# The channel loop of an attention and state-space backward pass: another order for the first roundings, the exponentials and the correlation copies, and two Toeplitz tiles

## The chip, the cores and the metric

The kernel runs on one core of a Trainium2 chip. A core has engines that each work through a queue of their own and meet through semaphores: TensorE (PE: matrix products, with the loading of weights shown apart as PEld), VectorE (DVE), ScalarE (ACT), GpSimd (POOL), and SyncE (SP), which here issues the DMAs. On-chip memory is SBUF; matrix products land in PSUM, which is cut into 8 banks of 128 x 512 fp32 values. The metric is the device time of one execution in microseconds (us), the median of several.

## The reference

A block mixes attention (without a causal mask) and a state-space convolution (S4) with a gate per token; asked for are its value and the gradients of twelve of its inputs, given grad_out. Everything but the S4 parameters is bfloat16. Cut to what is computed:

```python
def fwd(x, wqkv, wo, A, Bc, Cc, log_dt, Dskip, gate_w):    # A, Bc, Cc complex [576, 128]
    g = sigmoid((x * gate_w).sum(-1, keepdims=True))
    q, k, v = heads(x @ wqkv)                                # 2048 tokens, 32 heads of 18
    a = merge(softmax(q @ k.T * 18**-0.5) @ v) @ wo
    dt = exp(log_dt)
    K = real(sum_n(Cc * exp(dt * A * l) * (dt * Bc)))        # l = 0..2047, one K per channel
    y = causal_convolution(u, K) + u * Dskip                 # u: its own input, with x's data
    return g * a + (1 - g) * y
out, vjp = jax.vjp(fwd, ...)
return (out, *vjp(grad_out))
```

Here u is a constant: the gradient through it isn't asked for.

## The kernel before

The program has five stages: projections and preparation, attention forward and backward, the attention gradients' last products, the S4 part (from L708 on), and a final stage that puts the outputs together. The change touches the S4 part and, for one row, the final stage.

**What the S4 part computes.** The sequence of 2048 is cut into 16 pieces of 128 positions. Per channel there are 128 complex modes. For each channel the powers exp(dt A l), l from 0 to 127, are made as a 128 x 128 table E1e (real and imaginary part). With it, TensorE turns the inputs and the gated output gradients of each piece into states (uvp, copied to UV), a recurrence over the 16 pieces carries states forward and adjoint states backward (HG), a second product brings them back to positions (ybp), and what happens inside a piece is a Toeplitz product with the channel's kernel (T0w). Sums over products of states (pairs1, pairs2) give the parameter gradients, and the correlation of x with the output gradient inside a piece goes along two further columns of RX into the same states.

**How it is staged.** The 576 channels go in NBLK = 18 blocks of CB = 32, each block in two halves (h = 0, 1) of GS = 16 channels, and each half in 4 groups (q) of 4 channels, since 4 channels x 128 modes fill one PSUM bank. The loop is a software pipeline: `for i in range(-1, NBLK + 1)` works in one iteration on the recurrence of block i, the tables of block i + 1, the Toeplitz part of block i - 1, the masks and correlation products of block i + 3 (`mb`) and their collection for block i + 2 (`sb`).

The functions that the prediction names:

- `phase` (L856): one matmul `ph` of 3 rows of split phases (`thr`) with the positions (`lrow`), into one of three PSUM banks with the tag "ph".
- `ex` (L863): per half four phases, each turned to its exponential `ab` by ScalarE (L867). The exponentials need another function table than the roundings before them (ACT_TABLE_LOAD). Both halves of block i + 2 are made at the end of iteration i, into the two `ab` tiles.
- `kk` (L869): a phase, which ScalarE rounds by adding the constant MAGIC (L874). `ff` (L876): VectorE subtracts phase and rounding, which leaves the fraction of a turn. The phase's bank is free only after that. There is one `kk` tile.
- `sn` (L881): sine and cosine of the fractions on ScalarE. `prod` (L889): the products E1e of these with `ab` on VectorE (L892, L893), and a DMA transpose to E1n.
- `uv` (L897): the state matmuls uvp into two banks with the tag "uv", copied to UV by ScalarE.
- `scan` (L913): the recurrence HG on VectorE, 15 steps. It begins with a cast (L918), with which one iteration is told from the next in the trace.
- `kp` (L967): the Toeplitz kernel's row of every channel, stored to Kp_d. `t0` (L1013): per half the load of T0w from Kp_d (L1023), 16 matmuls `tps` into the bank with the tag "tm", and on VectorE the sum `yd` (L1028) with `ydi`.
- `load_rx`, `prep_rx` (L776, L784): for every second block the load of the columns RX and of `gob`, and three products by VectorE (L786, L788, L789).
- `m_load` (L791): the load of `xs` and `gyp` for the correlation, and 7 copies of xs shifted by 1 to 7 partitions, from SBUF to SBUF (L796). `m_mask` (L798): their masks on VectorE (L801). `m_part` (L803): products `psM`, also in the bank "tm", copied by ScalarE to `mst` (L812) and stored to Md_d by four DMAs each. `m_skw` (L823): four skewed loads from Md_d. `m_sum` (L831): four matmuls with `sel` into the bank "misc". `m_fin` (L836): three copies by ScalarE of the result, the last into the row dDs_row.
- `pairs2` (L996): products by VectorE (pq, rr), summed by TensorE over k with an identity, also into "misc" (58 matmuls `misc<-rr,ident_bf`). `sums` (L1010): ScalarE's copy SS of the result.

Of the 8 banks, "ph" has three, "uv" two, and "misc", "ybp" and "tm" one each.

**What sets the order.** On TensorE, ScalarE, VectorE and GpSimd the order is that of the program text (L770). The DMAs of SP are put in order by the framework's scheduler, and each waits in SP's queue until what it reads is there and what it overwrites is free.

Of the kernel before, what the change touches and what calls it, by code (L numbers as in the profile page):

```python
# [10 lines left out]
ACT = mybir.ActivationFunctionType  # L11
BF = mybir.dt.bfloat16
F32 = mybir.dt.float32
# [4 lines left out]
P = 128  # L18


def build(tc, aps, dbg_aps=None, stages=("s1", "attn", "post", "s4", "final")):
    nc = tc.nc
# [16 lines left out]
    S, D = x2.shape  # L39
# [21 lines left out]
    with ExitStack() as gctx:  # L61
# [27 lines left out]
        N = A_re.shape[1]  # L89
# [618 lines left out]
        if "s4" in stages:  # L708
            CB = 32
# [5 lines left out]
            s4c = s4c_cm.__enter__()  # L715
            SS = s4c.tile([P, 6, D], F32, name="SS")
            CK = s4c.tile([P, 2, 2, D], BF, name="CK")
            dDs_row = s4c.tile([1, D], F32, name="dDs_row")
            ones_f = s4c.tile([P, 1], BF, name="ones_f")
            nc.vector.memset(ones_f, 1.0)  # L720

            with ExitStack() as ctx:
# [80 lines left out]
                def m_part(b, u):  # L803
                    d0 = b * CB
                    psM = pps.tile([P, 4, P], F32, tag="tm", name="psM")
                    for q in range(4):
                        for g_ in range(4):
                            dd = u * 16 + 4 * q + g_
                            mm(psM[32 * g_:32 * (g_ + 1), q, :].rearrange("p (a b) -> p a b", b=SUB), lhsT=gyp[:, :, dd],
                               rhs=xs[:, :, ::-1, dd], tile_position=(0, 32 * g_))  # L810
                    mst = mst2[u]
                    nc.scalar.copy(mst[:, :, 0:P], psM)  # L812
                    for g_ in range(4):
                        dst = Md_d[d0 + u * 16:d0 + (u + 1) * 16].rearrange("(q g) t w -> g t q w", g=4)
                        nc.sync.dma_start(dst[g_], mst[32 * g_:32 * g_ + SUB, :, :])
# [20 lines left out]
                def m_fin(b):  # L836
                    RX = RXs[b // 2][0]
                    o = (b % 2) * CB
                    pk = dkp(b)
                    nc.scalar.copy(RX[:, CDK, o:o + CB], pk)  # L840
                    nc.scalar.mul(RX[:, CDK + 1, o:o + CB], pk, l0col)
                    nc.scalar.copy(dDs_row[:, b * CB:(b + 1) * CB], pk[0:1, :])

                def blk(b):
                    if b not in BK:
# [7 lines left out]
                                nc.sync.dma_start(t_[32 * (1 - r_):32 * (1 - r_) + 3, :], spl_d[r_, :, dG:dG + GS, :].rearrange("q d n -> q (d n)"))  # L853
                    return BK[b]

                def phase(b, h, q, which):  # L856
                    B_ = blk(b)
                    r0 = 32 * which
                    ph = pps.tile([P, 4, N], F32, tag="ph", bufs=3, name="ph")
                    mm(ph.rearrange("p c n -> p (c n)"), lhsT=lrow[r0:r0 + 3, :], rhs=B_["rw"][h][r0:r0 + 3, q * 4 * N:(q + 1) * 4 * N], tile_position=(r0, 0))  # L860
                    return ph

                def ex(b, h):  # L863
                    B_ = blk(b)
                    ab = B_["ab"][h] = pw.tile([P, GS, N], F32, tag="ab", bufs=2, name="ab")
                    for q in range(GS // 4):
                        nc.scalar.activation(ab[:, 4 * q:4 * q + 4, :], phase(b, h, q, 1), ACT.Exp)  # L867

                def kk(b, h, q):  # L869
                    B_ = blk(b)  # L870
# [142 lines left out]
                def t0(b, h):  # L1013
# [3 lines left out]
                        ydx[b // 2] = pw.tile([P, 2, NB, XB], BF, tag="yd", name="yd")  # L1017
                    yd = ydx[b // 2]
                    RX = RXs[b // 2][0]
                    T0w = pw.tile([P, GS, P], BF, tag="T0w", name="T0w")  # L1020
                    dh = b * CB + h * GS
                    src = bass.AP(tensor=Kp_d.tensor, offset=Kp_d[dh:dh + 1, 1:2].offset, ap=[[1, P], [2 * P, GS], [1, P]])
                    nc.sync.dma_start(T0w, src)  # L1023
# [21 lines left out]
                m_fin(0)  # L1045
                m_part(1, 0)
                m_part(1, 1)
                for i in range(-1, NBLK + 1):
                    cur = 0 <= i < NBLK
                    nx = i + 1 < NBLK  # L1050
                    mb = i + 3 if i + 3 < NBLK else None
                    sb = i + 2 if i + 2 < NBLK else None
                    if mb is not None:
                        m_load(mb)
                    if nx:
                        kk(i + 1, 0, 0); kk(i + 1, 0, 1)
                    if cur:
                        scan(i, 0, 3)
                    if nx:
                        ff(i + 1, 0, 0); kk(i + 1, 0, 2)  # L1060
                    if sb is not None:
                        m_skw(sb)
                    if cur:
                        scan(i, 3, 5)
                    if nx:
                        ff(i + 1, 0, 1); kk(i + 1, 0, 3)
                    if cur:
                        scan(i, 5, 7)
                    if nx:
# [6 lines left out]
                    if cur:  # L1076
                        scan(i, 9, 15)
                        casts(i)
                        rw1(i)
                    if sb is not None and sb % 2 == 0:  # L1080
                        load_rx(sb // 2)
                    if i >= 1:
                        t0(i - 1, 0)
                        t0(i - 1, 1)
                    if sb is not None and sb % 2 == 0:
                        prep_rx(sb // 2)
                    if nx:
                        prod(i + 1, 0)
                        kk(i + 1, 1, 0); kk(i + 1, 1, 1); kk(i + 1, 1, 2)
# [13 lines left out]
                        kp(i)  # L1103
                    if mb is not None:
                        m_mask(mb)
                    if nx:
                        prod(i + 1, 1)
                        uv(i + 1, 1)
                    if cur:
                        pairs2(i)  # L1110
                    if sb is not None:
                        m_sum(sb)
                        m_fin(sb)
                    if i + 2 < NBLK:
                        ex(i + 2, 0)
                        ex(i + 2, 1)
                    if cur:
# [7 lines left out]
        if "final" in stages and "s4" in stages:  # L1125
            out0_v = aps_out["out_0"][0].rearrange("(t p) d -> p t d", p=P)
            out1_v = aps_out["out_1"][0].rearrange("(t p) d -> p t d", p=P)
            with ExitStack() as ctx:
# [84 lines left out]
                nc.vector.tensor_copy(rowb, row)  # L1213
                nc.sync.dma_start(aps_out["out_10"].rearrange("(o d) -> o d", o=1), rowb)
                rowb2 = pf.tile([1, D], BF, name="ddsrowb")
                nc.vector.tensor_copy(rowb2, dDs_row)
                nc.sync.dma_start(aps_out["out_11"].rearrange("(o d) -> o d", o=1), rowb2)

# [105 lines left out]
```

## Time and profile before

| | |
|---|---|
| time, median of 3 runs | 4279.74 us (4272.59 to 4279.76) |
| the profiled execution's own time | 4279.8 us |
| its span, first to last instruction | 4278.1 us |
| granted TensorE clock, mean | 0.561 |
| busy in the span: PE, DVE, ACT | 3258.8, 2934.7, 2930.1 us |
| the loop from the first HG cast to the last | 2986.75 to 4053.64 us of the span |
| DMA traffic over the span | 521 MB, mean 122 GB/s |

The page gives, of one execution, the busy time of each engine, the span in 40 slices, the DMA queues, and the costliest groups of instructions. The slices show the stages: the span up to slice 27 of 40 is attention and the products behind it, the rest the S4 part and the final stage. Each digit is a busy share in tenths:

```
PE   8979999999999999999999999693334344334311
DVE  5527767777777777677677778022767767767878
```

In the trace's views, a group row has a line, an engine, an operation and its tiles (out<-in), the count, the busy time and mean length, and the idle time of the engine just ahead of it with what ended it. A row of the list of waits says who waited for whom, the sum, how often, and the longest. In a timeline each row has a start, a length, and in brackets the idle time ahead.

### The profile page before, as it was taken

To read this page: it belongs to the slowest core of one execution; us is meant where nothing else is said; L and a number is where in the kernel's file an instruction comes from. 1 tells how busy PE (TensorE), PEld (TensorE's weight loads), DVE (VectorE), ACT (ScalarE), POOL (GpSimd) and SP (SyncE) were. 2 spreads that over 40 slices of the span, in tenths; PEclk is the share of its full clock that TensorE was granted. 3 is DMA by queue.
4 is the path that set the end of the run, shared out by engine and by line. 5 is a ranking of instruction groups with operands and counts; after the bars stand their busy time and mean duration, and the time that the engine had idled before them with its cause. 6 is when DMAs were issued, how large, how long until landed. Compare 5 with 4: busy or idle time off the path is not lost. (4 is left out here: it accounts for less than half of the span.)

```text
span 4278.1 us, 64835 instructions
## 1 busy us (share of the span) xinstructions
PE 3258.8 (76%) x24562; PEld 1156.9 (27%) x24562; DVE 2934.7 (69%) x5147; ACT 2930.1 (68%) x5340; POOL 21.7 (1%) x45
## 2 busy tenths in 40 slices
PE   8979999999999999999999999693334344334311
PEld 2312222222222222222222222362223223223310
DVE  5527767777777777677677778022767767767878
ACT  4469989989989899899899897013555455455501
POOL 0000000000000000000000000000000000000000
PEclk9855555555555555555555555795555555555555
DMA  7446777677777767776767777774454444454347
GB/s 196 144 100 122 126 137 119 126 136 122 124 136 122 134 129 124 135 125 124 137 122 120 129 120 137 208 180 81 80 95 88 87 89 86 86 95 85 71 124 174
DMA packets 1789270, 521.42 MB, mean 122 GB/s; under 512 B 1702074, under 2 KB 1767684, under 8 KB 1788956
## 3 DMA queue, kind: packets, MB, share of 16 engines
q1 hardware_dynamic: 1788956, 517.27, 62.6%
q8 instruction: 193, 3.16, 0.3%
q14 instruction: 121, 0.99, 0.1%
HBM read 102.10 MB, written 60.96 MB: 38 GB/s over the span
## 5 line engine op out<-in xcount | busy, mean ns | idle before, releaser
L604 DVE TENSOR_TENSOR ds<-ps_P,PT 128x512 bf16<-128x512 f32 x2048 | 1329.8, 687 | 468.9 <-PE ps_P L30 262.1
L595 ACT ACTIVATE PT<-ps_P 128x512 bf16<-128x512 f32 x2048 | 1226.3, 603 | 141.5 <-PE ps_P L30 87.4
L599 ACT ACTIVATE eb<-ps_P 128x512 bf16<-128x512 f32 x2048 | 1235.9, 605 | 19.5 <-PE ps_P L30 19.0
L30 PE MATMUL ps_P<-dOaT,VaT_g 19*128 19x512 bf16 x2048 | 1196.4, 601 | 27.6 <-DMA VaT_g<-VaT_d 25.9
L30 PE MATMUL ps_P<-KaT_g,QaT_g 19*128 19x512 bf16 x2048 | 1161.5, 591 | 7.6 <-ACT PT L595 7.6
L30 PE MATMUL ps_P<-QaT_g,KaT_g 19*128 19x512 bf16 x2048 | 1055.9, 616 | 10.1 <-DMA KaT_g<-KaT_d 6.1
L30 PE MATMUL accO<-PT,Vtok_g 128*32 128x512 bf16 x2048 | 333.2, 632 | 0.0
L30 PE MATMUL tps<-RX,T0w 128*128 128x32 bf16 x576 | 38.5, 235 | 377.7 <-DMA T0w<-Kp_d 328.9
L30 PEld LDWEIGHTS <-KaT_g 19*128 19x128 bf16 x2048 | 138.2, 105 | 691.4 <-issue 664.5
L30 PE MATMUL accK<-dsT,Qtok_g 128*32 128x256 bf16 x4096 | 316.5, 407 | 2.1 <-DVE dqa L481 1.2
L30 PEld LDWEIGHTS <-VaT_g 19*128 19x128 bf16 x2048 | 198.6, 99 | 433.7 <-issue 404.2
L30 PE MATMUL accQ<-ds,Ktok_g 128*32 128x512 bf16 x2048 | 267.8, 621 | 1.2 <-DVE dvacc L464 1.1
L30 PE MATMUL accV<-eb,dOa 128*32 128x512 bf16 x2048 | 267.8, 621 | 0.6 <-DVE dkacc L505 0.6
L874 ACT ACTIVATE kk<-ph,magc 128x512 f32<-128x512 f32 x144 | 91.2, 688 | 207.9 <-DVE E1e L892 204.4
L30 PE MATMUL uvp<-RX,E1e 128*128 128x64 bf16 x1152 | 134.4, 291 | 122.9 <-DVE E1e L893 122.9
L879 DVE SCALAR_TENSOR_TENSOR kk<-kk,ph 128x512 f32<-128x512 f32 x144 | 95.1, 682 | 170.0 <-ACT kk L874 170.0
L30 PEld LDWEIGHTS <-QaT_g 19*128 19x128 bf16 x2048 | 176.6, 99 | 50.7 <-issue 27.5
L30 PE MATMUL ph<-thr,lrow 3*128 3x512 bf16 x288 | 136.7, 568 | 69.5 <-ACT ab L867 22.3
L481 DVE TENSOR_TENSOR dqa<-dqa,accQ 128x512 f32<-128x512 f32 x224 | 153.8, 687 | 49.1 <-PE accQ L30 48.8
L464 DVE TENSOR_TENSOR dvacc<-dvacc,accV 128x512 f32<-128x512 f32 x224 | 154.1, 688 | 36.0 <-PE accV L30 15.8
L30 PEld LDWEIGHTS <-E1e 128*128 128x128 bf16 x1152 | 126.1, 122 | 143.3 <-DVE E1e L893 142.2
L30 PE MATMUL ybp<-Rw,E1n 128*128 128x31 bf16 x1152 | 70.1, 233 | 103.2 <-ACT ydi L965 100.5
(279 smaller groups left out, 3558.3 us busy)
## 6 DMA issues: line engine op xcount, KB each, us to landing
T0w<-Kp_d SPq DMA_DIRECT2D x36, 512.0 KB
dsT<-ds SPq DMA_TRANSPOSE x512
dqkv_d<-dtk SPq DMA_DIRECT2D x96, 72.0 KB
dqkv_tok<-dqkv_d SPq DMA_DIRECT2D x1, 6912.0 KB
Md_d<-mst SPq DMA_DIRECT2D x144, 36.0 KB
ga_d<-ga_st SPq DMA_DIRECT2D x16, 288.0 KB
dxm_d<-dxm SPq DMA_DIRECT2D x16, 288.0 KB
skw<-Md_d SPq DMA_DIRECT2D x72, 64.0 KB
```

What stands on the lines that cost most here:

```text
L30: return nc.tensor.matmul(out, lhsT=lhsT, rhs=rhs, start=start, stop=stop, **kw)
L464: nc.vector.tensor_tensor(a_, a_, acc, op=A.add)
L481: nc.vector.tensor_tensor(U["dqa"], U["dqa"], acc, op=A.add)
L595: nc.scalar.activation(U["PT"][i][:, j, :], ps, ACT.Exp)
L599: nc.scalar.activation(e, ps, ACT.Exp)
L604: nc.vector.tensor_tensor(U["ds"][i][:, j, :], ps, U["PT"][i][:, j, :], op=A.mult)
L874: nc.scalar.activation(B_["kk"][h][:, 4 * q:4 * q + 4, :], ph, ACT.Identity, bias=magc, scale=1.0)
L879: nc.vector.scalar_tensor_tensor(v_, v_, MAGIC, B_["ph"].pop((h, q)), op0=A.subtract, op1=A.subtract)
```

## The change

The change reorders the end and the beginning of an iteration and gives two things another place:

- The exponentials' phases go into the two banks "uv" instead of the three "ph".
- The phases and roundings of groups 0 to 2 of block i + 2's first half are written ahead of the exponentials at the end of iteration i (for block 0 ahead of the loop), where they were written one by one at the beginning of iteration i + 1. Group 3 follows the first subtraction `ff`.
- `m_load` comes behind the second subtraction, no longer first in the iteration.
- T0w gets two buffers. `load_rx` comes behind `t0`, and `prep_rx` behind `m_mask`, ahead of the second half's products.
- `m_sum` and `m_fin` come ahead of `pairs2`. The third copy of `m_fin` goes into a small tile `dds` and by a DMA per block to a row in DRAM, `dDs_d`; the final stage loads that row.

```diff
-            dDs_row = s4c.tile([1, D], F32, name="dDs_row")
+            dDs_d = dram.tile([1, D], F32, name="dDs_d")
...
-                    nc.scalar.copy(dDs_row[:, b * CB:(b + 1) * CB], pk[0:1, :])
+                    dds = pw.tile([1, CB], F32, tag="dds", bufs=2, name="dds")
+                    nc.scalar.copy(dds, pk[0:1, :])
+                    nc.sync.dma_start(dDs_d[:, b * CB:(b + 1) * CB], dds)
...
-                def phase(b, h, q, which):
+                def phase(b, h, q, which, tag="ph", bufs=3):
                     B_ = blk(b)
                     r0 = 32 * which
-                    ph = pps.tile([P, 4, N], F32, tag="ph", bufs=3, name="ph")
+                    ph = pps.tile([P, 4, N], F32, tag=tag, bufs=bufs, name="ph")
...
-                        nc.scalar.activation(ab[:, 4 * q:4 * q + 4, :], phase(b, h, q, 1), ACT.Exp)
+                        nc.scalar.activation(ab[:, 4 * q:4 * q + 4, :], phase(b, h, q, 1, "uv", 2), ACT.Exp)
...
-                    T0w = pw.tile([P, GS, P], BF, tag="T0w", name="T0w")
+                    T0w = pw.tile([P, GS, P], BF, tag="T0w", bufs=2, name="T0w")
...
+                kk(0, 0, 0); kk(0, 0, 1); kk(0, 0, 2)
                 for i in range(-1, NBLK + 1):
...
-                    if mb is not None:
-                        m_load(mb)
-                    if nx:
-                        kk(i + 1, 0, 0); kk(i + 1, 0, 1)
                     if cur:
                         scan(i, 0, 3)
                     if nx:
-                        ff(i + 1, 0, 0); kk(i + 1, 0, 2)
+                        ff(i + 1, 0, 0); kk(i + 1, 0, 3)
...
-                        ff(i + 1, 0, 1); kk(i + 1, 0, 3)
+                        ff(i + 1, 0, 1)
+                    if mb is not None:
+                        m_load(mb)
...
-                    if sb is not None and sb % 2 == 0:
-                        load_rx(sb // 2)
                     if i >= 1:
                         t0(i - 1, 0)
                         t0(i - 1, 1)
                     if sb is not None and sb % 2 == 0:
-                        prep_rx(sb // 2)
+                        load_rx(sb // 2)
...
                     if mb is not None:
                         m_mask(mb)
+                    if sb is not None and sb % 2 == 0:
+                        prep_rx(sb // 2)
                     if nx:
                         prod(i + 1, 1)
                         uv(i + 1, 1)
-                    if cur:
-                        pairs2(i)
                     if sb is not None:
                         m_sum(sb)
                         m_fin(sb)
+                    if cur:
+                        pairs2(i)
                     if i + 2 < NBLK:
+                        kk(i + 2, 0, 0); kk(i + 2, 0, 1); kk(i + 2, 0, 2)
                         ex(i + 2, 0)
                         ex(i + 2, 1)
...
+                dDs_row = pf.tile([1, D], F32, name="dDs_row")
+                nc.sync.dma_start(dDs_row, dDs_d)
```

ScalarE's order at the end of one iteration and the beginning of the next, before. RX and dDs_row are the three copies of `m_fin`, ab the exponentials, SS the copy of `sums`, mst those of `m_part`, kk the roundings:

```order
L972 CAST KT<-misc 32x128
L911 ACTIVATE UV<-uvp 128x64x8 x4
L840 CAST RX<-misc 128x32
L841 ACTIVATE RX<-misc,l0col 128x32
L842 COPY dDs_row<-misc 1x32
L867 ACT_TABLE_LOAD
L867 ACTIVATE ab<-ph 128x512 x8
L1011 COPY SS<-misc 128x6x32
L812 COPY mst_39425<-psM 128x4x128
L812 COPY mst_39427<-psM 128x4x128
L874 ACTIVATE kk<-ph,magc 128x512 x4
```

The same place in the changed kernel, where lines are up to two further down:

```order
L974 CAST KT<-misc 32x128
L913 ACTIVATE UV<-uvp 128x64x8 x4
L840 CAST RX<-misc 128x32
L841 ACTIVATE RX<-misc,l0col 128x32
L843 COPY dds<-misc 1x32
L876 ACTIVATE kk<-ph,magc 128x512 x3
L869 ACT_TABLE_LOAD
L869 ACTIVATE ab<-ph 128x512 x8
L1013 COPY SS<-misc 128x6x32
L812 COPY mst_39425<-psM 128x4x128
L812 COPY mst_39427<-psM 128x4x128
L876 ACTIVATE kk<-ph,magc 128x512
```

Three of the four roundings moved ahead of the table load; the fourth stays behind the mst copies.

SP's queue from the store of a block's Toeplitz rows on, before: the T0w loads, the stores of mst, the loads and shifted copies of xs (one row per shift, three of the seven shown here), and the skewed loads.

```order
L973 DMA Kp_d<-KT 32x128
L1023 DMA T0w<-Kp_d 128x16x128
L815 DMA Md_d<-mst_39425 16x4x144 x4
L815 DMA Md_d<-mst_39427 16x4x144 x4
L793 DMA xs<-in_A_x_dram 128x16x32
L794 DMA gyp<-in_grad_out_dram 128x16x32
L829 DMA skw<-Md_d 128x1x128 x2
...
L796 DMA xs<-xs 122x512
L796 DMA xs<-xs 121x512
L829 DMA skw<-Md_d 128x1x128 x2
L1023 DMA T0w<-Kp_d 128x16x128
```

The same place in the changed kernel, in an iteration with a load of gob ahead:

```order
L781 DMA gob<-in_grad_out_dram 128x16x64
L975 DMA Kp_d<-KT 32x128
L897 DMA_TRANSPOSE E1n<-E1e 128x32x128
L844 DMA dDs_d<-dds 1x32
L1025 DMA T0w<-Kp_d 128x16x128 x2
L815 DMA Md_d<-mst_39425 16x4x144 x4
L815 DMA Md_d<-mst_39427 16x4x144 x4
L829 DMA skw<-Md_d 128x1x128 x2
L793 DMA xs<-in_A_x_dram 128x16x32
L829 DMA skw<-Md_d 128x1x128 x2
L794 DMA gyp<-in_grad_out_dram 128x16x32
L796 DMA xs<-xs 127x512
```

The second T0w load moved from behind the shifted copies to directly behind the first; all four skewed loads now stand ahead of the shifted copies, two of them ahead of the load of xs; and the store of dDs_d is new.

VectorE's order in an iteration with RX products, before, from the end of the recurrence (wa, wb) to the first half's E1e products:

```order
L944 TENSOR_TENSOR wa<-HG,par 128x1920
L944 TENSOR_TENSOR wb<-HG,par 128x1920
L1028 TENSOR_TENSOR yd<-tps,ydi_39429 128x32x16 x2
L786 TENSOR_TENSOR RX<-gob,omg_t 128x1024
L788 TENSOR_SCALAR RX<-RX,l1col 128x960
L789 TENSOR_SCALAR RX<-RX,l0col 128x960
L892 TENSOR_TENSOR E1e<-kk,ab 128x16x128
```

And around the RX products in the changed kernel:

```order
L985 TENSOR_TENSOR rr<-pq 128x480
L799 TENSOR_TENSOR gyp<-gyp,omp 128x512
L801 TENSOR_SCALAR xs<-xs,msk 128x512 x7
L786 TENSOR_TENSOR RX<-gob,omg_t 128x1024
L788 TENSOR_SCALAR RX<-RX,l1col 128x960
L789 TENSOR_SCALAR RX<-RX,l0col 128x960
L894 TENSOR_TENSOR E1e<-kk,ab 128x16x128
```

They moved from behind the two yd sums to behind the masks xs, ahead of the second half's E1e products.

## The prediction

> **What bounds the kernel now.** I read the page's forty slices first: up to about 2,900 us TensorE is full, after that no engine is, and that stretch is the channel loop, where alone the change lies. Two views then say who sets its pace, both from the first HG cast to the last (17 iterations): the busy times by window and the list of waits. The window row gives start and end, length, then busy us of PE, PE's weight loads, DVE, ACT and POOL, the clock, the DMA share and GB/s. A wait row gives who waited for whom, the total, how often, and the longest.
>
> ```profile
> 2986.75:4053.64 1066.89, 444.13 (x5094) 317.20 (x5094) 780.82 (x1383) 560.11 (x796) 0.00 (x0) 0.57 0.46 86
> ...
> DVE kk L879 <- ACT kk L874: 161.3, 34, 9.2
> DVE yd L1028 <- PE tps L30: 81.2, 16, 6.5
> DVE RX L788 <- DMA RX<-xr_d: 13.3, 7, 2.0
> ```
>
> VectorE works 780.8 of 1066.9 us. These three waits come to 255.8; smaller waits and gaps of a few hundredths between instructions make up the other 30. So the loop goes at the pace of VectorE's queue, whose work is done in the order written, and a wait shortened there shortens the loop, until the next wait on the same queue takes its place. ScalarE (560) and the DMA engines (0.46 of the window; the same bytes in some 905 us would be 0.54) have room. The timeline of VectorE in one iteration without an RX step (3427.46 to 3489.23), and a row of the next one, shows where the waits sit. Columns are start, length, line and instruction, and in brackets the idle time ahead of it and what ended it:
>
> ```profile
> 3427.46 0.22 DVE L918 CAST HG<-UV 128x128 f32<-128x128 bf16 x1
> ...
> 3429.62 0.29 DVE L928 TENSOR_TENSOR HG<-tz 128x128 f32<-128x128 f32 x1
> 3438.32 0.69 DVE L879 SCALAR_TENSOR_TENSOR kk<-kk,ph 128x512 f32<-128x512 f32 x1 [8.42 <-ACT kk L874]
> ...
> 3441.03 0.68 DVE L879 SCALAR_TENSOR_TENSOR kk<-kk,ph 128x512 f32<-128x512 f32 x1
> ...
> 3446.43 0.68 DVE L879 SCALAR_TENSOR_TENSOR kk<-kk,ph 128x512 f32<-128x512 f32 x1
> ...
> 3457.84 0.68 DVE L1028 TENSOR_TENSOR yd<-tps,ydi 128x512 bf16<-128x512 f32 x1
> 3463.83 0.69 DVE L1028 TENSOR_TENSOR yd<-tps,ydi 128x512 bf16<-128x512 f32 x1 [5.31 <-PE tps L30]
> 3464.44 2.28 DVE L892 TENSOR_TENSOR E1e<-kk,ab 128x2048 bf16<-128x2048 f32 x1
> ...
> 3474.00 0.69 DVE L879 SCALAR_TENSOR_TENSOR kk<-kk,ph 128x512 f32<-128x512 f32 x1 [1.14 <-ACT kk L874]
> ...
> 3489.23 0.22 DVE L918 CAST HG<-UV 128x128 f32<-128x128 bf16 x1
> ...
> 3530.05 0.47 DVE L788 TENSOR_SCALAR RX<-RX,l1col 128x960 bf16<-128x960 bf16 x1 [2.04 <-DMA RX<-xr_d]
> ```
>
> From here t is us after the cast at 3427.46. Of the 34 waits for kk, 17 are long, like the 8.42, and 17 short, like the 1.14. The short ones (19 us) stay, since everything around the second half's subtractions keeps its order. The long ones make 142.
>
> **Part 1: roundings, phases, correlation copies.** What the first subtraction waits for stands on ScalarE and TensorE. Their timelines in the same iteration, with one sel row of another one and the group row of the exponentials (busy us, mean ns, idle):
>
> ```profile
> 3429.07 0.19 ACT L840 CAST RX<-misc 128x32 bf16<-128x32 f32 x1 [2.78 <-PE misc L30]
> ...
> 3429.51 1.28 ACT L867 ACT_TABLE_LOAD   x1
> 3430.80 4.04 ACT L867 ACTIVATE ab<-ph 128x512 f32<-128x512 f32 x8
> 3434.66 0.38 ACT L1011 COPY SS<-misc 128x192 f32<-128x192 f32 x1
> 3435.15 0.59 ACT L812 COPY mst<-psM 128x512 f32<-128x512 f32 x1
> 3437.02 0.59 ACT L812 COPY mst<-psM 128x512 f32<-128x512 f32 x1 [1.28 <-PE psM L30]
> 3437.60 1.84 ACT L874 ACTIVATE kk<-ph,magc 128x512 f32<-128x512 f32 x3
> 3439.68 0.69 ACT L874 ACTIVATE kk<-ph,magc 128x512 f32<-128x512 f32 x1 [0.24 <-PE ph L30]
> ...
> L867 ACT ACTIVATE ab<-ph 128x512 f32<-128x512 f32 x144 | 73.0, 627 | 27.8 <-PE ph L30 27.6
> ```
>
> ```profile
> 3421.91 3.75 PE L30 MATMUL uvp<-RX,E1e 128*128 128x64 bf16 x32
> 3425.48 0.92 PE L30 MATMUL misc<-rr,ident_bf 128*128 128x32 bf16 x30
> ...
> 3428.00 1.04 PE L30 MATMUL misc<-sel,skw 128*128 128x8 f32 x8
> ...
> 3431.45 2.54 PE L30 MATMUL ph<-thr,lrow 3*128 3x512 bf16 x5 [1.03 <-ACT ab L867]
> ...
> 3439.07 0.58 PE L30 MATMUL ph<-thr,lrow 3*128 3x512 bf16 x1 [0.71 <-DVE kk L879]
> ...
> 3556.14 1.85 PE L30 MATMUL misc<-sel,skw 128*128 128x8 f32 x8
> ```
>
> Before, all four roundings stand behind the table load, eight exponentials, SS and two mst copies, 8.1 us of ScalarE (3429.51 to 3437.60). Three of them moved ahead of these, the chain runs thus. uvp ends at t -1.80 (3425.66). The sel matmuls, now directly behind it, take 1.04 to 1.85: -0.76 at best. m_fin's three copies take 0.44 (3429.07 to 3429.51): -0.32. A wait is new here: the first rr matmul of pairs2 must wait for the last of these copies, since both use the misc bank. Behind it on TensorE stand all 58 rr matmuls, the three phases and then everything else, and ScalarE waits for the phases. At 0.92 for 30 the 58 take 1.78: 1.46. A phase 0.58, a rounding 0.69: 2.7. VectorE is ready at 2.45 (3429.62 + 0.29), so its first subtraction waits 0.3, or 1.1 with slow sel matmuls, where it waited 8.42.
>
> The fourth rounding stays behind the mst copies, and that is **what is late next**. The third rounding ends at 2.04 + 1.84 = 3.9, and with the load's 1.28 the exponentials start at 5.2. With three banks eight of them took 4.04, one each 0.49 (0.63 for the last alone). In the two uv banks a bank turns around in 0.58 (phase) + 0.63 (exponential) + 0.03 (hand-overs, as 3439.07 + 0.58 to 3439.68) = 1.24 for two, so eight take 3 x 1.24 + 0.49 + 0.63 = 4.84. No row shows eight in two banks. The ends are 4.04, no loss, and 8 x 1.24 = 9.9, one bank at a time. I take 4.84: it is nearest to the five phases of the quoted row, which follow the exponentials without further idle time. The last exponential then starts at 9.4, when its phase is done. From the last phase's end the first mst copy comes 1.16 later (3433.99 to 3435.15): 10.6. The second comes 1.87 after that, the rounding 0.58 later, and takes 0.69: 13.7, or 14.5 with slow sel. Unhindered, the fourth subtraction would stand at 2.45 + 3 x 2.71 (3438.32 to 3441.03) = 10.6. So 3.1 to 3.9 us of waiting per iteration remain, both waits together; I take 3.5, 16 times, and 0.5 in the last, which has no psM ahead. Left: 56.5 of 142, **gain 86**.
>
> Here a rule speaks against moving work next to the table load. The row has 1.28, and the exponential starts 0.01 after it. The Trainium skill's page "ScalarE: Activation LUTs", section "What ACT_TABLE_LOAD costs", puts a switch at about 2.66 us, the load and a drain of 1.38. By it the fourth rounding would come 1.38 later and the gain be 22 smaller, 4140 in all. The trace disagrees: no drain fits between the two rows.
>
> **Part 2: two T0w tiles.** The second yd waits for its matmuls, these for T0w. Rows of SP's queue, of TensorE, and of VectorE near the loop's end:
>
> ```profile
> 3429.05 0.39 SPq L1023 DMA_DIRECT2D T0w<-Kp_d  x1
> 3439.53 0.60 SPq L793 DMA_DIRECT2D xs<-in_A_x_dram  x1
> ...
> 3453.28 1.30 SPq L829 DMA_DIRECT2D skw<-Md_d  x2
> 3454.68 0.41 SPq L1023 DMA_DIRECT2D T0w<-Kp_d  x1
> 3455.14 5.05 SPq L853 DMA_DIRECT2D thr<-spl_d  x2
> ...
> 3462.72 1.07 PE L30 MATMUL tps<-RX,T0w 128*128 128x32 bf16 x16 [22.07 <-DMA T0w<-Kp_d]
> ...
> 3973.92 0.69 DVE L1028 TENSOR_TENSOR yd<-tps,ydi 128x512 bf16<-128x512 f32 x1 [1.16 <-PE tps L30]
> ```
>
> The second load was issued 25.6 behind the first, after the shift copies, and landed 8.04 later. Now both go out at t 2 to 4, behind Kp_d's landing and the new dDs_d store. An issue directly behind a T0w is held up by some 5 us, so SP is free by 9, before the first mst copy ends at 11 and has stores for it. Even at 8.04 each the tiles land by 12 and 20. They are wanted at 13 (the first half's matmuls, behind the mst copies on TensorE) and at 26. Next late is the bank: the second half's matmuls wait until the first yd has read it, and behind them on TensorE stand only phases and uvp that wait for later VectorE work anyway. That price is in the trace, in the last iterations of the loop, where no shift copies run: 1.16. So 16 x 1.16 = 19 of 81.2 stay, **gain 62**. If the loads stayed late, nothing.
>
> **Part 3: RX products behind the masks, RX load behind the t0 loads.** The products' 2 us of work only move. The load goes out behind the shift copies and the second half's matmuls at about t 32, and even with T0w's 8.04 lands at 40; it is wanted at 43: **gain 13**; uncovered, 0. In these iterations the next gob load waits on SP for the first product (t 44), with the Kp_d store and an E1n transpose behind it; what these store is made later, so nobody waits.
>
> The dDs copy keeps its length; its 18 stores of one row and the one load lie beside a waiting SP. Start-up, the last T0w pair and the final stage change by a microsecond or so with both signs: nothing. That m_load is written later moves SP's queue alone; see rival 3.
>
> **Sum**: 85.4 + 62.6 + 13.3 = 161.3, off the profiled execution's 4279.8 (span 4278.1 and what lies around it; the median of the runs is 4279.74, so no correction): 4118.5, put down as **4118 us**.
>
> **Rivals.**
> 1. *The ScalarE chain is longer* than worked out and the fourth subtraction later. With one bank at a time it is 5.1 x 16 = 81 more, 4199; halfway 4160. For it: no row shows two banks here. Against: the hand-overs of 0.03. A pause behind the table load as long as the load itself would add 16 x 1.28 = 20, 4138; the rows show none.
> 2. *T0w's second load stays late*, so that the edit doesn't do what it says: 62 back, 4180. Against: on SP's queue both stand together.
> 3. *The shift copies become the bound*, the case that ends slower:
>
> ```profile
> 2930.86 0.61 SPq L793 DMA_DIRECT2D xs<-in_A_x_dram  x1
> ...
> 2950.27 0.84 DVE L801 TENSOR_SCALAR xs<-xs,msk 128x512 bf16<-128x512 bf16 x2 [2.30 <-DMA xs<-xs]
> ...
> 3477.03 1.92 DVE L801 TENSOR_SCALAR xs<-xs,msk 128x512 bf16<-128x512 bf16 x7
> ```
>
> Before, masks came 37.5 after the xs load's issue, without waiting. The start-up, where VectorE does wait for them, shows that the last copies take 19.4 from that issue. The load was issued 1.92 after the second mst copy's end, and two skw loads (1.30) now stand ahead of it: 13.0 + 1.92 + 1.3 = 16.2, all copies landed at 35.6. E1e starts at 14.1 + 11.4 (3446.43 to 3457.84) + 1.84 + 0.61 (two yd) = 28, the masks 12.6 later (3464.44 to 3477.03), the last two at 42. The slack is 6. Each us beyond it costs 15 in all. Copies that land 16 later than reckoned eat the whole gain, about 10 per iteration, and from there on the kernel is slower: at 20, 4280 + 4 x 15 = 4340.
>
> **How the numbers follow.** Forecast 0.62, with its own bounds 4098 (better hand-overs and short sel) to 4131; ScalarE chain longer 0.15; a pause behind the load 0.02; T0w late 0.07; shift copies 0.10, of which 0.04 end slower and 0.02 level; better than all this 0.04. From 4090 to 4182 some 0.14 are left out: the worse end of rival 1 and the worse half of rival 3. About 0.2% is what a measurement of this kernel can tell from no change. Faster 0.94, same 0.02, slower 0.04.
>
> **What would show it.** Right: per iteration the first subtraction waits under 1.2 us, the fourth about 3, the second yd 1.16, RX and the masks not at all; iterations last about 53 us, with RX 55. Rival 1 shows as 6 to 8 at the fourth subtraction, rival 2 as 5 at the second yd, rival 3 as a wait of xs for DMA. I am wrong if VectorE's waits in the loop exceed 130 us, or if VectorE's instructions themselves grow.

## The result and the profile after

The changed kernel takes **4098.64 us** (median of 4 runs, 4097.04 to 4100.78) against 4277.77 for the kernel before (4 runs, 4272.59 to 4279.76): a ratio of 0.9583, 95% interval 0.9567 to 0.9600. The forecast was 4118 with a range from 4090 to 4182. The profiled execution took 4099.21, its span is 4097.5, 180.6 less than before.

Where the time came from is read from the same two views as before, from the first HG cast to the last: the busy times by window and VectorE's list of waits (lines are up to two further down than before).

```profile
2983.77:3874.99 891.22, 433.76 (x5097) 312.04 (x5098) 780.49 (x1384) 564.40 (x796) 0.00 (x0) 0.57 0.56 103
```

```profile
DVE kk L881 <- ACT kk L876: 61.8, 34, 2.8
DVE yd L1030 <- PE tps L30: 18.5, 16, 1.2
DVE HG L920 <- ACT UV L913: 4.4, 1, 4.4
DVE E1e L894 <- ACT kk L888: 4.2, 2, 2.1
```

The loop is 891.2 long instead of 1066.9, 175.7 less, and VectorE's work in it is the same to 0.3 us. The three waits of before account for all of it: kk 161.3 to 61.8 (99.5), yd 81.2 to 18.5 (62.7), RX 13.3 to nothing: 175.5. Another 2 us went behind the loop and 3 ahead of it.

VectorE's timeline in one iteration without an RX step:

```profile
3351.36 0.22 DVE L920 CAST HG<-UV 128x128 f32<-128x128 bf16 x1
...
3353.72 0.68 DVE L881 SCALAR_TENSOR_TENSOR kk<-kk,ph 128x512 f32<-128x512 f32 x1
...
3364.42 0.69 DVE L881 SCALAR_TENSOR_TENSOR kk<-kk,ph 128x512 f32<-128x512 f32 x1 [2.53 <-ACT kk L876]
...
3375.83 0.68 DVE L1030 TENSOR_TENSOR yd<-tps,ydi 128x512 bf16<-128x512 f32 x1
3377.67 0.69 DVE L1030 TENSOR_TENSOR yd<-tps,ydi 128x512 bf16<-128x512 f32 x1 [1.16 <-PE tps L30]
...
3390.87 1.92 DVE L801 TENSOR_SCALAR xs<-xs,msk 128x512 bf16<-128x512 bf16 x7
...
3403.07 0.22 DVE L920 CAST HG<-UV 128x128 f32<-128x128 bf16 x1
```

The first subtraction stands 2.36 after the cast and doesn't wait; the fourth waits 2.53, the second yd 1.16, the masks not at all, and the iteration lasts 51.7. ScalarE's timeline at the same place shows what the fourth waits for:

```profile
3350.63 0.16 ACT L843 COPY dds<-misc 1x32 f32<-1x32 f32 x1
3352.79 1.84 ACT L876 ACTIVATE kk<-ph,magc 128x512 f32<-128x512 f32 x3 [2.01 <-PE ph L30]
3354.66 1.28 ACT L869 ACT_TABLE_LOAD   x1
3355.95 1.09 ACT L869 ACTIVATE ab<-ph 128x512 f32<-128x512 f32 x2
...
3359.75 1.10 ACT L869 ACTIVATE ab<-ph 128x512 f32<-128x512 f32 x2 [0.18 <-PE ph L30]
3360.75 0.30 ACT L1013 COPY SS<-misc 128x192 f32<-128x192 f32 x1
3361.33 0.59 ACT L812 COPY mst<-psM 128x512 f32<-128x512 f32 x1 [0.28 <-PE psM L30]
3363.21 0.59 ACT L812 COPY mst<-psM 128x512 f32<-128x512 f32 x1 [1.29 <-PE psM L30]
3363.69 0.69 ACT L876 ACTIVATE kk<-ph,magc 128x512 f32<-128x512 f32 x1
```

The roundings begin 1.43 after the cast, the exponentials 4.59, and they end at 9.5; then SS, the two mst copies with TensorE's psM between them, and the fourth rounding. On TensorE the sel matmuls, the rr matmuls and the first phases ran ahead of the roundings, and on SP both T0w loads went out together:

```profile
3349.09 1.24 PE L30 MATMUL misc<-sel,skw 128*128 128x8 f32 x8
3350.84 1.60 PE L30 MATMUL misc<-rr,ident_bf 128*128 128x32 bf16 x58 [0.51 <-ACT dds L843]
3352.37 0.87 PE L30 MATMUL ph<-thr,lrow 3*128 3x512 bf16 x5
```

```profile
3351.16 1.73 SPq L1025 DMA_DIRECT2D T0w<-Kp_d  x2
```

### The profile page after: what moved, and what is told of

It is laid out like the page before. It is cut to its first block, busy times and chain, and to the rows that moved or that the text cites. A ratio compares the mean times of both kernels' runs of the same rounds, so it can differ in the third digit from the quotient of the medians.

```text
span 4097.5 us, 64890 instructions
## 1 busy us (share of the span) xinstructions
PE 3242.8 (79%) x24562; PEld 1146.9 (28%) x24562; DVE 2931.2 (72%) x5147; ACT 2934.7 (72%) x5340; POOL 21.7 (1%) x45
## 5 line engine op out<-in xcount | busy, mean ns | idle before, releaser
L30 PE MATMUL ph<-thr,lrow 3*128 3x512 bf16 x288 | 126.2, 570 | 86.6 <-ACT ab L869 59.8
L913 ACT ACTIVATE UV<-uvp 128x512 bf16<-128x512 f32 x144 | 86.0, 597 | 84.8 <-PE uvp L30 84.8
```

Source lines behind the costliest of these rows:

```text
L30: return nc.tensor.matmul(out, lhsT=lhsT, rhs=rhs, start=start, stop=stop, **kw)
L913: nc.scalar.mul(UV[:, ri, :, c0:c0 + 8], pr, -1.0 if ri == 0 else 1.0)
```

## The experiments

The forecast added three parts: 85.4 for part 1 (roundings, phases, correlation copies), 62.6 for part 2 (T0w), 13.3 for part 3 (RX). That the sum came out doesn't show that each part is worth its term. So parts were taken out of the changed kernel one by one, and put alone into the kernel before. The theory behind most of the expectations (A) is that a wait taken away lets VectorE come sooner to the next thing that isn't ready; the rival (B) that each part has its own price wherever it stands. Times are medians; each run was timed in turn with the kernel before, at 4275 to 4278 us.

### One T0w tile

```diff
-                    T0w = pw.tile([P, GS, P], BF, tag="T0w", bufs=2, name="T0w")
+                    T0w = pw.tile([P, GS, P], BF, tag="T0w", name="T0w")
```

> The changed kernel with one T0w tile again. Theory A (waits replace each other): the second T0w load again goes out behind the seven shifted copies, which the changed kernel finishes issuing 29 us after the HG cast; with the 8 us that it took before to land and 1 us of matmuls the second yd stands at 38, where VectorE is ready at 25.5. So it waits some 12 to 13 instead of 1.16, 11 more in each of 16 iterations: 177 back, about 4276 us, with yd waits of about 200 in the loop. Theory B (the prediction's rival 2, parts add up): only the 62 us of this part come back, about 4161 us, yd waits about 81.

Measured: **4278.2 us**, ratio to before 1.0007 (0.9998 to 1.0017). Without the second tile the whole change is worth nothing. The list of waits, and rows of SP's queue, of TensorE and of VectorE in one iteration (cast at 3431.35):

```profile
DVE yd L1030 <- PE tps L30: 197.0, 16, 15.1
```

```profile
3441.87 3.66 SPq L815 DMA_DIRECT2D Md_d<-mst  x8
...
3450.59 9.90 SPq L796 DMA_DIRECT2D xs<-xs  x7
3460.60 0.55 SPq L1025 DMA_DIRECT2D T0w<-Kp_d  x1
```

```profile
3469.08 1.07 PE L30 MATMUL tps<-RX,T0w 128*128 128x32 bf16 x16 [24.23 <-DMA T0w<-Kp_d]
```

```profile
3455.80 0.69 DVE L1030 TENSOR_TENSOR yd<-tps,ydi 128x512 bf16<-128x512 f32 x1
3470.19 0.69 DVE L1030 TENSOR_TENSOR yd<-tps,ydi 128x512 bf16<-128x512 f32 x1 [13.70 <-PE tps L30]
```

The second load goes out 29.3 after the cast, and the second yd stands at 38.8, later than the 36.4 of before. What part 1 gained is waited for here. Theory A holds.

### Part 1 alone, part 2 alone, part 3 alone

The kernel before with part 1 (the lines of the change above but for T0w, dDs and RX):

> The kernel before with part 1 alone: early roundings, exponentials' phases in the uv banks, correlation copies ahead of pairs2, load of xs written later; one T0w tile, RX load and products where they were. Theory A: the first subtraction's 8.4 us are gone, but the second yd stands at the landing of the second T0w, 38 to 39 us after the cast (36.4 before), and the RX product behind it waits 2 to 5 more: iterations as in the run with one T0w tile, plus that in 8 of them: slower than before, about 4294 to 4318 us, yd waits about 200. Theory B (parts add up): 99 us of kk waits gone, about 4177 us.

Measured: 4294.04, ratio 1.0043 (1.0028 to 1.0058): **slower**. Its list of waits:

```profile
DVE yd L1028 <- PE tps L30: 198.0, 16, 15.1
DVE kk L879 <- ACT kk L874: 62.3, 34, 2.8
DVE RX L788 <- DMA RX<-xr_d: 13.4, 7, 2.1
```

The 99 us of kk waits are gone as in the changed kernel, and 117 have come at the second yd. A was right in the sign and in the yd waits; the RX waits did not grow, so the time is at the lower end.

Part 2, with the dDs row in DRAM:

```diff
-            dDs_row = s4c.tile([1, D], F32, name="dDs_row")
+            dDs_d = dram.tile([1, D], F32, name="dDs_d")
...
-                    T0w = pw.tile([P, GS, P], BF, tag="T0w", name="T0w")
+                    T0w = pw.tile([P, GS, P], BF, tag="T0w", bufs=2, name="T0w")
```

> The kernel before with two T0w tiles and the dDs row in DRAM (whose place in SBUF the second tile needs), nothing else. Theory A (parts take each other's waits): the second yd waits 1.16 instead of 5.3 to 6.5, 62 in all; VectorE then comes to the RX product 4 to 5 us earlier, while its load, behind the shifted copies, can move up by some 3 only and takes 4 to 7: the RX waits grow from 13 to between 17 and 45. About 4218 to 4246 us. Theory B (parts add up): 62 off, RX waits as before, about 4214 us.

Measured: 4209.4, ratio 0.9844 (0.9830 to 0.9859). Here B holds:

```profile
DVE kk L881 <- ACT kk L876: 161.6, 34, 9.3
DVE yd L1030 <- PE tps L30: 18.5, 16, 1.2
DVE RX L788 <- DMA RX<-xr_d: 13.7, 7, 2.1
```

The loop lost 62.0 us, from 1066.9 to 1004.9; the rest of the 67 lies ahead of it and behind it. The RX load goes out when the second half's tps have been computed, in the kernel before (tps done at 3526.15, load issued at 3526.18) and here, and these came earlier by as much as VectorE did. So the RX waits stayed.

Part 3, the two RX steps moved as in the change:

```diff
-                    if sb is not None and sb % 2 == 0:
-                        load_rx(sb // 2)
...
                     if sb is not None and sb % 2 == 0:
-                        prep_rx(sb // 2)
+                        load_rx(sb // 2)
...
                         m_mask(mb)
+                    if sb is not None and sb % 2 == 0:
+                        prep_rx(sb // 2)
```

> The kernel before with part 3 alone: load of RX behind the t0 loads, its products behind the masks. Theory A (a wait that stands behind the second yd, with nothing late next): the 13 us of RX waits go, the yd and kk waits stay at 81 and 161: 13 faster, about 4262 us. Theory B (alone it is hidden, as the loop's chain goes from one yd to the next): no change, 4275 us.

Measured: 4263.18, ratio 0.9964 (0.9953 to 0.9975), no RX wait in the list, kk 163.8 and yd 81.6: its 13 us, as reckoned. Alone the three parts come to +17, -67 and -14, -64 in all; together to -179.

### RX steps put back

The changed kernel with the two steps where they were (the diff just shown, backwards).

> The changed kernel with the load of RX ahead of the t0 loads and its products behind the yd sums again. Theory A (waits replace each other): the load goes out behind the shifted copies, 29 us after the cast, and lands 4 us later as before, at 33; VectorE would be at the product that needs it at 28: 5 us of waiting in each of 8 iterations, 40 slower, about 4139 us. Theory B (parts add up): the 13 us of before come back, about 4112 us.

Measured: 4151.97, 53 slower than the changed kernel. The list, SP's queue and VectorE (cast at 3426.62):

```profile
DVE RX L788 <- DMA RX<-xr_d: 58.7, 7, 9.0
```

```profile
3456.16 0.64 SPq L779 DMA_DIRECT2D RX<-xr_d  x1
```

```profile
3463.33 0.47 DVE L788 TENSOR_SCALAR RX<-RX,l1col 128x960 bf16<-128x960 bf16 x1 [8.21 <-DMA RX<-xr_d]
```

A in its mechanism: now the load waits on SP for the shifted copies, no longer for the tps, and goes out at 29.5, with VectorE due at 28.5. The size was low, since it took 7.2 from issue to the product where 3.9 was reckoned: the same part is worth 14 in the kernel before and 53 here.

### Late roundings

```diff
-                kk(0, 0, 0); kk(0, 0, 1); kk(0, 0, 2)
                 for i in range(-1, NBLK + 1):
...
+                    if nx:
+                        kk(i + 1, 0, 0); kk(i + 1, 0, 1); kk(i + 1, 0, 2)
                     if cur:
                         scan(i, 0, 3)
...
-                        kk(i + 2, 0, 0); kk(i + 2, 0, 1); kk(i + 2, 0, 2)
                         ex(i + 2, 0)
```

> The changed kernel with the three roundings written at the beginning of the iteration again, behind exponentials, SS and both mst copies; exponentials stay in the uv banks. Theory A (the rounding's place is what part 1 is worth): the exponentials begin at 1.7 and end at 6.6 after the cast, the second mst copy ends at 9.6, the first subtraction stands at 10.3 where VectorE is ready at 2.45: it waits 7.9, the fourth not at all, in place of 2.65: 5.2 x 16 = 83 slower, about 4182 us. Theory B (ScalarE has the same work up to the last rounding either way, and that alone counts): no change, 4099 us.

Measured: 4185.97, 87 slower. The list of waits, and VectorE in an iteration with the cast at 3390.93:

```profile
DVE kk L881 <- ACT kk L876: 152.3, 34, 8.9
```

```profile
3400.92 0.69 DVE L881 SCALAR_TENSOR_TENSOR kk<-kk,ph 128x512 f32<-128x512 f32 x1 [7.55 <-ACT kk L876]
```

Theory A holds. ScalarE's work up to the fourth rounding is the same either way, but in the changed kernel three subtractions and their scan steps run beside the exponentials.

### The exponentials' banks

```diff
-                        nc.scalar.activation(ab[:, 4 * q:4 * q + 4, :], phase(b, h, q, 1, "uv", 2), ACT.Exp)
+                        nc.scalar.activation(ab[:, 4 * q:4 * q + 4, :], phase(b, h, q, 1), ACT.Exp)
```

> The changed kernel with the exponentials' phases in the three ph banks again. Theory A (the banks matter): the three early roundings hold these banks until their subtractions (ends 3.0, 5.75 and 8.4 us after the cast), so the third exponential can start at 9.0 only and the eight end at about 12.1 instead of 9.7; the fourth subtraction waits 5 instead of 2.65: 2.4 x 16 = 38 slower, about 4137 us. Theory B (the order of the roundings does it all, another bank is free in time): no change, 4099 us.

Measured: 4110.94, 12 slower, so neither. The list of waits, and ScalarE with the cast at 3407.90:

```profile
DVE kk L881 <- ACT kk L876: 77.4, 39, 3.6
```

```profile
3411.48 1.28 ACT L869 ACT_TABLE_LOAD   x1
3412.78 0.60 ACT L869 ACTIVATE ab<-ph 128x512 f32<-128x512 f32 x1
3414.04 1.08 ACT L869 ACTIVATE ab<-ph 128x512 f32<-128x512 f32 x2 [0.67 <-PE ph L30]
```

A had let the phases take the three banks in turn, and the third wait for the third subtraction. That subtraction began at 3415.75, when three exponentials were under way or done: the third did not wait for it. The second phase began at 3413.43, right behind the end of the first exponential (3413.38) and ahead of the end of the second subtraction (3413.73), so it took the first one's bank again. The exponentials lose 0.67 once, at the second, and the kk waits in the list are 77.4, 15.6 more: the idle banks are worth 12 us.

### Correlation copies behind pairs2

```diff
+                    if cur:
+                        pairs2(i)
                     if sb is not None:
                         m_sum(sb)
                         m_fin(sb)
-                    if cur:
-                        pairs2(i)
```

> The changed kernel with the sel matmuls and the three copies of m_fin behind pairs2 again. Theory A (the chain to the fourth rounding is what counts): the sel matmuls end about 2.0 after the cast, the copies at 2.45, and the roundings, which began at 1.65, begin there: 0.8 later, and so does the fourth: 0.8 x 16 = 13 slower, about 4112 us. Theory B (the place of the copies matters only by the bank they share): no change, 4099 us.

Measured: 4112.4, 14 slower, with 13.8 us more of kk waits in the list:

```profile
DVE kk L881 <- ACT kk L876: 75.6, 49, 2.8
```

Theory A holds in the size. The wait comes in two places: in the iteration that was read, the roundings begin 2.16 after the cast, the first subtraction now waits 0.44, and the fourth 2.83.

### The load of xs first, and the masks early

m_load in its old place, first in the iteration:

```diff
+                    if mb is not None:
+                        m_load(mb)
                     if cur:
                         scan(i, 0, 3)
...
                         ff(i + 1, 0, 1)
-                    if mb is not None:
-                        m_load(mb)
```

> The changed kernel with m_load written first in the iteration again. Theory A (its place moves SP's queue alone, and the shifted copies have time): the xs load goes out some 1.3 us earlier, nobody waits for it: no change, 4099 us. Theory B (its later place is a part of the gain, since SP's queue is what T0w and RX wait in): slower by 0.5 us or more per iteration, 4107 us or above, with waits of the second yd or of RX.

Measured: 4097.09; from first to last cast the loop took 891.96, 0.7 more than in the changed kernel. Theory A holds: no difference that this measurement could tell.

The masks earlier, to learn what the shifted copies have to spare:

```diff
                         rw2(i)
+                    if mb is not None:
+                        m_mask(mb)
...
-                    if mb is not None:
-                        m_mask(mb)
```

> The changed kernel with the masks of gyp and xs written 6 us earlier, behind rw2 and ahead of the second half's subtractions: it measures how much the shifted copies have to spare. Theory A (the slack of the prediction's rival 3, about 6 us): the last copies land 19.4 after the xs load's issue as in the start-up, 35.2 after the cast; the last masks would stand at 35: xs waits below 0.5 per iteration. Theory B (in the loop the copies share the DMA engines and land later): they land at about 38 and the masks wait 2.5 to 3.5, 40 to 56 us in all. In both the masks no longer cover the second half's sines: the second sine ends 3.8 after the last subtraction, pq and rr take 1.8, so E1e waits 2 in the iterations without RX products, 16 in all. A: 4115 to 4123 us; B: 4155 to 4171 us.

Measured: 4115.15, the low end of A. From its list of waits:

```profile
DVE kk L881 <- ACT kk L876: 50.1, 37, 2.8
DVE E1e L894 <- ACT kk L888: 20.3, 17, 2.1
DVE yd L1030 <- PE tps L30: 18.5, 16, 1.2
DVE xs L801 <- DMA xs<-xs: 4.6, 6, 2.1
```

The edit moved the masks by 5 us, not 6: behind the loop's first iteration they begin about 34.5 after the cast instead of 39.6. They wait in 4 of the 15 iterations that have masks, 4.6 us in all, 2.1 of it in the first, so the copies are just in time. What costs more is that the sines are uncovered, E1e 20.3 where it was 4.2. Theory A left out that the masks now cover part of the second half's roundings: the kk waits fell by 11.7. VectorE's recorded work was 3.5 longer and the loop 13.1 in all, so that the time met the low end of A is partly luck.

### What is late next, taken away

First the correlation products behind the fourth rounding:

```diff
-                        ff(i + 1, 0, 0); kk(i + 1, 0, 3)
+                        ff(i + 1, 0, 0); kk(i + 1, 0, 3)
+                    if pb is not None:
+                        m_part(pb, 0)
+                        m_part(pb, 1)
...
-                    if mb is not None:
-                        m_part(mb, 0)
-                        m_part(mb, 1)
```

(`pb` is i + 2 from iteration 0 on, the block whose masks the iteration before has made.)

> The changed kernel with the correlation products psM and their mst copies written behind the fourth rounding instead of ahead of it. Theory A (the fourth subtraction waits for the mst copies in ScalarE's queue, nothing else): that rounding begins 10.0 after the cast and its subtraction waits 0.2 instead of 2.65: 2.5 x 16 = 40 faster, about 4059 us. With it the xs load goes out 0.7 later and the masks come 2.5 earlier; by their landing in the changed kernel the last shifted copies have some 1 to 3 us to spare, so a wait of up to 1 us for xs may give 16 back (4075). Theory B (the exponentials' chain, not the copies, sets the fourth rounding): no change, 4099 us.

Measured: 4056.63, 42 faster than the changed kernel, ratio to before 0.9485 (0.9470 to 0.9501). The fourth rounding stands directly behind SS, and kk waits are 21.6:

```profile
DVE kk L881 <- ACT kk L876: 21.6, 22, 1.1
...
DVE RX L788 <- DMA RX<-xr_d: 1.6, 2, 1.4
```

Then, on top of it, the other waits in the list:

```diff
-                    ph = B_["ph"][(h, q)] = phase(b, h, q, 0)
+                    ph = B_["ph"][(h, q)] = phase(b, h, q, 0, *(("tm", 1) if (h, q) == (1, 3) else ("ph", 3)))
...
-                    tps = pps.tile([P, 2, NB, GS], F32, tag="tm", name="tps")
+                    tps = pps.tile([P, 2, NB, GS], F32, tag="uv" if h else "tm", bufs=2 if h else 1, name="tps")
...
-                        kk(i + 1, 1, 0); kk(i + 1, 1, 1); kk(i + 1, 1, 2)
+                        kk(i + 1, 1, 0); kk(i + 1, 1, 1); kk(i + 1, 1, 2); kk(i + 1, 1, 3)
...
-                        ff(i + 1, 1, 0); kk(i + 1, 1, 3)
+                        ff(i + 1, 1, 0)
...
-                    if sb is not None and sb % 2 == 0:
-                        prep_rx(sb // 2)
                     if nx:
                         prod(i + 1, 1)
                         uv(i + 1, 1)
+                    if sb is not None and sb % 2 == 0:
+                        prep_rx(sb // 2)
```

> The run with the correlation products behind the fourth rounding (4056.6 us), with what its trace leaves of waits taken away: the second half's tps in an uv bank (yd waits 18.5 there), the fourth rounding of the second half with its phase in the tm bank, ahead of the state matmuls (short kk waits 19), RX products behind the second half's E1e (RX waits 1.6). Theory A (VectorE's queue is still all that counts): 38 faster, about 4018 us, waits of VectorE in the loop about 10, iterations near 47. Theory B (a transfer or ScalarE's chain is late next): most of it comes back as waits for xs, T0w, RX or E1e, 4035 to 4057 us.

Measured: **4016.57** (5 runs, 4013.31 to 4021.53), ratio to before 0.9397 (0.9384 to 0.9409), faster than both kernels. The loop and its waits:

```profile
2986.42:3795.11 808.69, 419.37 (x5097) 311.65 (x5097) 776.88 (x1383) 559.78 (x796) 0.00 (x0) 0.61 0.64 113
```

```profile
DVE HG L920 <- ACT UV L913: 4.4, 1, 4.4
DVE E1e L894 <- ACT kk L888: 4.2, 2, 2.1
DVE xs L801 <- DMA xs<-xs: 1.3, 6, 0.4
```

VectorE works 776.9 of 808.7 us. Theory A holds; what is left in this loop is VectorE's work itself with the short gaps between its instructions, and the first sign of the shifted copies. The three moves were made together, and what each is worth is read from the list alone.

## Why the prediction was right, point by point

- **VectorE's queue sets the pace: right.** The window lost what three waits lost. With the correlation products behind the fourth rounding it lost 38.1 more for 38.6 us of waits, and in the last run another 44.4 for 40.4 of waits and 3.9 less recorded work of VectorE, the cause of which stays open.
- **Part 1: right in the mechanism, its size low by 14.** It took 85.4 for the kk waits, 99.5 went. The step is the 3.5 us of remaining wait per iteration, chosen between 3.1 and 3.9, half-way to slow sel matmuls. The list gives 2.65, below both: 61.8 less 17 short waits of 1.14, by 16. The roundings began at 1.43 to 1.65 after the cast, not 2.04: the sel matmuls ended in time in both iterations that were read, the 58 rr matmuls took 1.60 and the phases overlapped their end. The first subtraction doesn't wait at all, where 0.3 to 1.1 was reckoned. That the fourth rounding behind the mst copies is late next was right: moved ahead of them it gave 42 more.
- **Eight exponentials in two banks: right.** 4.84 was reckoned; from 3355.95 to the last one's end at 3360.85 they took 4.90.
- **The table load.** The rows above have 1.28 for it, the rounding's end at 3354.63 is 0.03 ahead and the exponential 0.01 behind. By the Trainium skill's page "ScalarE: Activation LUTs", section "What ACT_TABLE_LOAD costs", a drain of 1.38 belongs to each switch; the trace of the changed kernel doesn't agree either, and 4140 was not the time.
- **Part 2: right as a term of this sum, 62.6 reckoned and 62.7 gone.** The second yd waits 1.16, for its bank. With the second half's tps in another bank that wait went as well. One reading on the way did not hold, though nothing in the sum hung on it: that an issue directly behind a T0w is held up by some 5 us. In the changed kernel both T0w loads take 1.73 us of SP's queue, and thr loads that follow the shifted copies with no T0w between are held 4.39 (at 3381.36).
- **Part 3: right, 13.3 of 13.3.**
- **The sum: right within this change.** Of the 19 us that the forecast is too high, 14 are part 1's remaining wait. The rest lies outside the loop: the stages ahead of the S4 part, which the change doesn't touch, were 4 us shorter in this execution (their last cast, `dwo_bf`, stands at 2891.7 instead of 2895.7), the start-up was 1 longer, and what follows the loop 2 shorter.
- **Rival 2's price: wrong.** It put T0w's second load staying late at 62 us back, 4180. The run with one tile shows 179 back, 4278. The step that failed is that the price was taken from the waits of before, with VectorE coming to the second yd as late as it did then. The first yd stood 30.4 after the cast before and 24.5 in that run. The second load landed 2.5 later after the cast than before, mainly since the mst copies, and with them the shifted copies, come later: the stores of mst begin 10.5 after the cast, where they began at 8.3. So the whole gain hung on the second load going out early. The forecast gave the other case a chance of 0.07 and about a third of its cost, and part 1's term was right only because part 2 was there.
- **Rival 3: its slack was about right.** It was put at 6 us; masks moved 5 us ahead found the copies landed in 11 of 15 iterations and waited 4.6 us in the other four, of which 2.1 in the first. That the kernel would become slower beyond it wasn't tried.
- **Moves put at nothing: right** for m_load (0.7 us in the loop) and for the dDs store, behind which no wait appeared.

## What to carry to other kernels

Terms read from a list of waits added up here for edits made together; of the three parts alone, two kept their terms and the largest became a loss. Before a part is priced alone, or a rival by what happens without it, the walk must be made again with the engine arriving earlier: here one part alone cost 17, and a piece of it left out of the whole cost 87; a buffer worth 67 alone decided over 179.

On an engine that works in a written order, each wait is followed back to what stands ahead of its releaser in that queue, and that is moved; then the list is read again. Banks and buffers that are idle at that time are the cheap means. Work that waits for nothing is left where it covers another engine's chain, as the masks cover the sines.

## What the runs showed of the hardware that was not expected

A load's time from issue to use was no constant. In seven iterations of the kernel before, where other transfers stand between the RX load and the shifted copies on SP's queue, it took 3.7 to 3.9 us; in the one that was read, it was issued 10.5 us behind the last copy's issue. With the RX steps put back, directly behind the copies, it took 6.8 to 7.2 in seven iterations. The second T0w load behind the copies took 7.8 to 8.2 in the kernel before and 8.3 to 8.6 with one tile. Whether the copies' transfers or their issue hold these loads, or only how soon behind them they come, was not separated.
